# A planner's list that knows a shared SBUF path, and where the low parts of w_in are made

## The chip, the cores and the metric

One core of a Trainium2 chip runs the whole program in one launch. The metric is the device time in microseconds, the median over runs; three runs of the kernel before gave 571.86 us (569.98 to 573.15). The engines are TensorE (PE), VectorE (DVE), ScalarE (ACT), GpSimd (POOL) and SyncE (SP, which here only issues DMAs).

## The reference

For 4 batches of 8 heads, 576 tokens and 64 columns per head, the program computes causal attention and adds a linear-memory term, and then runs a two-layer network over all 2304 tokens:

```
scores = where(causal, -1e9, q @ k.T / sqrt(D));  a = exp(scores - max)
local  = (a / (a.sum(-1) + 1e-9)) @ v
q_p    = where(q > 0, q, exp(q) - 1) + 1
mem    = (q_p @ M_prev) / (q_p . z_prev + 1e-6)
x      = g * mem + (1 - g) * local            # g = sigmoid(beta), per head
out    = (s * relu(x @ w_in)**2 + b) @ w_out  # 512 -> 2048 -> 512
```

The weights come as 64-bit floats and are turned into 32-bit ones on the chip. Products with w_in and w_out use a high and a low part of each operand (three products in place of one).

## The kernel before

Sixteen pairs of heads (g = 0 to 15, four pairs to a batch) go through the same stages. For a pair, the scores of five row tiles (`scores`, L319) go to PSUM; `red` (L327, the instruction is at L330) adds the mask on VectorE, copies the tile to SBUF and keeps its extreme in `mn`; `ex` (L334, L336) is ScalarE's exponential, which leaves the row sum in `sm`; L367 adds 1e-9 to the sums and L368 takes reciprocals, both on VectorE; `scale` (L339, L342) multiplies each tile on GpSimd by its reciprocal and by 1 - g. Meanwhile `phi` (L262 to L292) makes the memory term's left side: two activations on ScalarE, a combination on VectorE (L275), a product with z on GpSimd (L277), its sum (L279), a small product and a reciprocal (L280, L283) on VectorE, and the normalised result on GpSimd (L287). TensorE then transposes the scaled tiles (`bank`, L383, instruction at L392), ScalarE and VectorE copy them out of PSUM (`copy`, L396 to L409), and the second product (`second`, L425, L435) yields x, which L456 (ScalarE) and L457 (VectorE) split into a high and a low part.

`convert` (L465) does w_in in 20 pieces of 128 rows, eight of 256 columns and twelve of 512. A piece is loaded by SP (L479); ScalarE takes the absolute value of the high word (L481); three VectorE instructions shift and merge the bits (L482, L483, L485); GpSimd makes the high part (L487); and the low part, the difference (L489), is made on GpSimd for the first 16 pieces (`WP = 16`) and on VectorE for the last four. Three raw buffers and two work buffers are taken in turn.

When a batch of x is there, `first` (L506) adds its products with w_in (L496 to L498), 41 tiles in all, as work that TensorE can do between the stages of later pairs. These use the full array ("full"), scores and transposes use it by rows ("row"), the second product by columns ("col").

The order of all this work is written by the class `Plan` (L42). Each step is added with its engine, an assumed cost, a rank, what it reads and writes and which PSUM buffers it takes and gives. `deal` (L72) plays the steps through with these costs: it keeps a clock for each engine, picks the engine that can start first and, of the steps that can start within 0.02 us, the one of lowest rank. For TensorE it keeps to the present kind of product, except that it leaves "full" when other work has waited `HOLD` us or amounts to `WORK` us. The steps are then issued in the order of their assumed starts, and each engine runs its instructions in that order, waiting at each for what it needs. Costs are only used for the order: the chip takes its own times. The copy's and the reduction's ranks are made earlier by UC and UR, and the ranks of the pieces are in `WRANK`.

After the last pair come the remaining products with w_in, and then the layer with w_out (L581 on), which the change does not touch.

Of the kernel before, what the change touches and what calls it, by code (L numbers as in the profile page):

```python
# [8 lines left out]
F32 = mybir.dt.float32  # L9
# [32 lines left out]
class Plan:  # L42
# [6 lines left out]
    RATE = 220.0e3  # L49
    SWITCH, HOLD, WORK = 0.14, 1.0, 2.0  # L50

# [3 lines left out]

    def add(self, eng, cost, fn, rank, reads=(), writes=(), take=(), give=(), bytes=0, mode=None, slack=0.0):
        s = dict(eng=eng, cost=cost, fn=fn, rank=rank, take=take, give=give, bytes=bytes, mode=mode, slack=slack,
                 n=len(self.steps), out=[], end=None)
        deps = {self.wrote[k]["n"]: self.wrote[k] for k in (*reads, *writes) if k in self.wrote}
        for k in writes:  # L60
            deps |= {r["n"]: r for r in self.read.pop(k, ())}
            self.wrote[k] = s
        for k in reads:
            self.read.setdefault(k, []).append(s)
        s["need"] = len(deps)
        s["deps"] = list(deps.values())
        for d in s["deps"]:
            d["out"].append(s)
        self.steps.append(s)
        return s  # L70

    def deal(self):  # L72
        ready = {}
        clock = {}
        wire = 0.0
        mode = None
# [10 lines left out]
        while any(ready.values()):  # L87
            best = None
            for eng, some in ready.items():
                t0 = clock.get(eng, 0.0)  # L90
                able = []
                for s in some:
                    t = max(t0, s["at"])
                    for place, pool in s["take"]:
                        if place is not None:
                            free = sorted(x for x in self.free[pool] if x is not None)
                            n = sum(1 for q in s["take"] if q[1] == pool)
                            t = max(t, free[n - 1] + s["slack"]) if len(free) >= n else None
                            break
                    if t is not None:  # L100
                        able.append((t, s))
# [21 lines left out]
            if s["eng"] == "PE":  # L123
                t += self.SWITCH * (s["mode"] != mode)
                mode = s["mode"]
            s["end"] = clock[s["eng"]] = t + s["cost"]
            if s["bytes"]:
                wire = max(wire, t) + s["bytes"] / self.RATE
                s["end"] = wire + 1.9
# [17 lines left out]
def attention_moe_kernel(  # L147
# [83 lines left out]
    NRM = two([128, 5, 2, 1], "nrm")  # L231
    MN, SM = two([128, 2, 5], "mn"), two([128, 2, 5], "sm")
    PR = two([128, 2, 1920], "P")
# [9 lines left out]
    def setup():  # L243
        nc.gpsimd.memset(mask, 0.0)
        for r, c in ((slice(0, 128), slice(448, 576)), (slice(0, 64), slice(576, 640)), (slice(64, 128), slice(576, 640))):
            nc.gpsimd.affine_select(
                out=mask[r, c], in_=mask[r, c], pattern=[[-1, c.stop - c.start]],
                compare_op=ALU.is_ge, fill=NEG, base=0, channel_multiplier=1,
            )
        nc.vector.memset(omg, 0.0)  # L250
        nc.scalar.activation(omg, omg, AF.Exp)
        for _ in range(WARM):
            nc.tensor.transpose(TB[3][:, :128], ident, ident)
# [5 lines left out]
    COLD, WARM = 1.2, 13  # L259
    UR, UC, UX = 0.6, 0.5, 1.0  # L260

    def phi(g):  # L262
# [11 lines left out]
        add("ACT", 0.72, lambda: nc.scalar.activation(q, q, AF.Exp), r0 + 0.61, [], [("q", u)])  # L274
        add("DVE", 0.80, lambda: nc.vector.scalar_tensor_tensor(q, q, 1.0, PHR, ALU.min, ALU.add), r0 + 0.7,  # L275
            ["phr"], [("q", u)])
        add(vec[0], 1.6 if own else 0.83, lambda: vec[1].tensor_mul(  # L277
            PHR, q, z.unsqueeze(1).to_broadcast([128, 5, 2, D])), r0 + 0.71, [("q", u), ("z", u)], ["phr"])
        add("DVE", 0.80, lambda: nc.vector.tensor_reduce(n, PHR, AX.X, ALU.add), r0 + 0.72, ["phr"], [("n", u)])  # L279
        add("DVE", 0.18, lambda: nc.vector.scalar_tensor_tensor(  # L280
            n, n, 1e-6, gin[:, hp:hp + 2].unsqueeze(1).unsqueeze(3).to_broadcast([128, 5, 2, 1]), ALU.add, ALU.mult),
            r0 + 0.73, ["gin"], [("n", u)])
        add("DVE", 0.2, lambda: nc.vector.reciprocal(n, n), r0 + 0.74, [], [("n", u)])  # L283

        def put(a, w, ts):
            o = P[:, :, a:].rearrange("q j (t c) -> q t j c", c=w)[:, :, :, 0:64]
            vec[1].tensor_mul(o, q[:, ts], n[:, ts].to_broadcast(list(o.shape)))  # L287

        add(vec[0], 0.85 if own else 0.5, lambda: put(0, 640, slice(2, 5)), r0 + 0.75, [("q", u), ("n", u)],
            [("phi", u, i) for i in (2, 3, 4)])  # L290
        add(vec[0], 0.62 if own else 0.4, lambda: put(384, 768, slice(1, None, -1)), r0 + 0.76, [("q", u), ("n", u)],
            [("phi", u, i) for i in (0, 1)])  # L292

    RED = (0.15, 0.27, 0.41, 0.54, 0.68)
    EXP = (0.34, 0.44, 0.55, 0.67, 0.77)
    SCL = ((0.38, 0.56, 0.7, 0.9, 0.96), (0.37, 0.5, 0.62, 0.78, 0.86))

    def attention(g):
# [3 lines left out]
        cold = 1.0 if own else COLD  # L302
        qk, P, mn, sm, V, xs = QK[u], PR[u], MN[u], SM[u], VS[u], XS[g % 8]
        add = plan.add
# [29 lines left out]
        def ex(i, j):  # L334
            pt = P[:, j, PB[i] + 64:PB[i] + 64 + QW[i]]
            nc.scalar.activation(  # L336
                pt, pt, AF.Exp, scale=-1.0, bias=mn[:, j, i:i + 1], accum_out=sm[:, j, i:i + 1])

        def scale(i, j):  # L339
            h = 2 * p + j  # L340
            pt = P[:, j, PB[i] + 64:PB[i] + 64 + QW[i]]
            nc.gpsimd.tensor_scalar(pt, pt, sm[:, j, i:i + 1], omg[:, h:h + 1], ALU.mult, ALU.mult)  # L342

# [5 lines left out]
        for v, group in enumerate(visits):  # L349
# [7 lines left out]
            for k, (i, o) in enumerate(tiles):  # L357
                for j in range(2):
                    last = k == len(tiles) - 1
                    add("DVE", RED[i], lambda i=i, j=j, o=o, ps=ps: red(i, j, o, ps), r + 0.1 + 0.01 * k - UR,  # L360
                        [("sc", g, v)], [("p", u, i, j), ("mn", u, i, j)], give=[(ps, j, "S")] if last else ())
                    add("ACT", EXP[i], lambda i=i, j=j: ex(i, j), r + 0.15 + 0.01 * k, [("mn", u, i, j)],
                        [("p", u, i, j), ("sm", u, i, j)])
            a, z = parts[v]
            keys = [("sm", u, i, j) for i in range(a, z) for j in range(2)]
            s = sm[:, :, a:z]
            add("DVE", 0.17, lambda s=s: nc.vector.tensor_scalar(s, s, 1e-9, None, ALU.add), r + 0.6, [], keys)  # L367
            add("DVE", 0.2, lambda s=s: nc.vector.reciprocal(s, s), r + 0.6, [], keys)  # L368
            for k, i in enumerate(i for i in (3, 1, 2, 0, 4) if a <= i < z):
                for j in range(2):  # L370
                    add("POOL", SCL[g >= 6][i], lambda i=i, j=j: scale(i, j), r + 0.7 + 0.01 * k,
                        [("sm", u, i, j), "omg"], [("p", u, i, j)])

# [37 lines left out]
        for q, k in enumerate((0, 3, 1, 2)):  # L411
# [6 lines left out]
            for h in range(2):  # L418
                add("DVE" if k == 3 else "ACT", 0.39 if k == 3 else 0.49, lambda k=k, h=h, ps=ps: copy(k, h, ps),
                    r + 0.1 - UC, [("tp", g, k)], [("pt", u if k > 1 else 2, h, k)], give=[(ps, h, "T")])  # L420
# [22 lines left out]
        for hi in (None,) if own else range(2):  # L443
# [3 lines left out]
            for n, (a, z) in enumerate(cuts):  # L447
# [4 lines left out]
                else:  # L452
# [4 lines left out]
                add("DVE", w + 0.03, lambda t=t, d=d: nc.vector.tensor_sub(d[:, 1], t(), d[:, 0].bitcast(F32)),  # L457
                    r0 + 2.3 - UX, [("av", g)] + key(0), key(1),
                    give=() if n < len(cuts) - 1 else [(ps, 0, "S") if own else (ps, hi, "T")])
# [5 lines left out]
    def convert(n):  # L465
# [7 lines left out]
        A, B_ = ("xa", n % 3), ("w", n % 2)  # L473
        k = (0.1 + 0.9 * n_ / 512)

        def add(eng, cost, *a):
            plan.add(eng, cost * k, *a)

        plan.add("SP", 0.06, lambda: nc.sync.dma_start(raw, words(w_in)[128 * p:128 * p + 128, c0:c0 + n_]),  # L479
                 rank - 3.0, writes=[A], bytes=1024 * n_)  # L480
        add("ACT", 0.65, lambda: nc.scalar.activation(w, hi.bitcast(F32), AF.Abs, scale=2.0 ** -112), rank, [A], [B_])  # L481
        add("DVE", 0.73, lambda: nc.vector.tensor_scalar(wu, wu, 3, None, ALU.logical_shift_left), rank, [], [B_])  # L482
        add("DVE", 0.95, lambda: nc.vector.scalar_tensor_tensor(  # L483
            wu, lo, 29, wu, ALU.logical_shift_right, ALU.bitwise_or), rank, [A], [B_])
        add("DVE", 0.72, lambda: nc.vector.scalar_tensor_tensor(  # L485
            wu, hi, 0x80000000, wu, ALU.bitwise_and, ALU.bitwise_or), rank, [A], [B_])
        add("POOL", 0.8, lambda: nc.gpsimd.tensor_scalar(H, w, 1.0, 1.0, ALU.mult, ALU.mult), rank, [B_], [("WH", n)])  # L487
        low = ("POOL", 1.35, nc.gpsimd) if n < WP else ("DVE", 0.8, nc.vector)
        add(*low[:2], lambda: low[2].tensor_sub(L, w, H.bitcast(F32)), rank, [B_, ("WH", n)], [("WL", n)])  # L489

# [43 lines left out]
    def flush():  # L534
# [4 lines left out]
    MM = [(b, f) for b in range(B - 1) for f in range(NF - LEFT * (b == 2))]  # L539
    WP = 16  # L540
    WRANK = [5.0, 6.6, 7.0, 7.2] + [9.0 + 0.2 * k for k in range(4)] + [10.0 + 0.2 * k for k in range(4)] + [
        12.0 + 0.6 * k for k in range(8)]

# [304 lines left out]
```

## Time and profile before

| | |
|---|---|
| Median of three runs | 571.86 us (569.98 to 573.15) |
| Profiled execution, time | 569.1 us |
| Profiled execution, span | 567.3 us |
| Mean granted clock of TensorE | 0.985 |
| Busy: PE / DVE / ACT / POOL | 543.0 / 357.0 / 398.4 / 319.7 us |
| L342 (scaling), GpSimd | 160 instructions, 113.1 us |
| L330 (reduction), VectorE | 160 instructions, 70.0 us |
| L336 (exponential), ScalarE | 160 instructions, 88.5 us |

The profiled execution lies at the lower end of the runs. Its busy times count an engine as busy while an instruction that it has begun waits for a resource, which matters where two engines share one. The span falls into the attention stage (to about 300 us) and the layer with w_out.

### The profile page before, as it was taken

The page shows a single profiled execution, that of the slowest core. Times are in us where ns is not written, and L with a number is a line of the kernel's source. Part 1 is how long each engine was busy: PE and PEld are TensorE (multiplying, and loading weights), DVE is VectorE, ACT ScalarE, POOL GpSimd, SP SyncE. Part 2 cuts the span into 40 slices and gives each one's busy share as a digit, 9 for nine tenths or more (in the row PEclk, how much of TensorE's full clock was granted, in tenths as well). Part 3 has the DMA queues.
Part 4 walks back from the last instruction along what each step waited for, and adds up shares of the span by engine and source line. Part 5 has one row for each costly group of instructions (what it writes and reads, how often), then busy time and mean ns, then how long its engine had stood idle before and what let it go on. Part 6 is the DMA issues. An engine that isn't in the chain of part 4 may idle for free.

```text
span 567.3 us, 11900 instructions
## 1 busy us (share of the span) xinstructions
PE 543.0 (96%) x4309; PEld 457.8 (81%) x4309; DVE 357.0 (63%) x868; ACT 398.4 (70%) x869; POOL 319.7 (56%) x341
## 2 busy tenths in 40 slices
PE   5987998999999999999999999999999999999996
PEld 4756765667777776777778888889999999999996
DVE  4887996897666544105305996346856886687562
ACT  5898876577787677226634675968789779877940
POOL 3699989985894665104400000143687687768850
PEclk9898998999999999999999999999999999999999
DMA  5635567573425443221119666648353535343101
GB/s 174 213 103 182 165 198 235 167 207 123 149 90 163 132 147 106 80 94 56 40 55 325 224 198 192 213 140 268 104 169 110 162 121 164 106 147 123 38 29 38
DMA packets 56666, 81.52 MB, mean 144 GB/s; under 512 B 7584, under 2 KB 39072, under 8 KB 56608
## 3 DMA queue, kind: packets, MB, share of 16 engines
q1 hardware_dynamic: 54592, 78.93, 43.5%
q10 hardware_dynamic: 2016, 1.84, 0.9%
q8 instruction: 34, 0.56, 0.4%
q14 instruction: 24, 0.20, 0.1%
HBM read 57.15 MB, written 23.59 MB: 142 GB/s over the span
## 4 chain that ended last, share of the span: by engine, by line
PE 64%; DVE 9%; POOL 9%; DMA 7%; ACT 7%; issue 3%; SPq 1%; ACTq 0%; POOLq 0%; DVEq 0%
PE yps L709 11%; PE yps L711 11%; PE yps L710 11%; PE tb L496 6%; PE sb L435 5%; PE sb L323 5%; PE tb L498 5%; PE tb L497 5%; DMA raw<-in_moe_w_out_dram 5%; POOL P L342 4%; PE tb L392 3%; DVE P L330 2%; ACT P L336 2%; POOL w0L L489 1%; DMA r_d<-r 1%
## 5 line engine op out<-in xcount | busy, mean ns | idle before, releaser
L342 POOL TENSOR_SCALAR P<-P,sm,omg 128x192 f32<-128x192 f32 (+4 forms) x160 | 113.1, 720 | 63.3 <-DVE sm L368 44.1
L336 ACT ACTIVATE P<-P,mn 128x64 f32<-128x64 f32 (+4 forms) x160 | 88.5, 562 | 24.1 <-DVE mn L330 23.9
L709 PE MATMUL yps<-bH,op 128*128 128x256 f32 x360 | 101.2, 281 | 0.0
L711 PE MATMUL yps<-bH,op 128*128 128x256 f32 x360 | 101.1, 281 | 0.0
L710 PE MATMUL yps<-bL,op 128*128 128x256 f32 x360 | 101.1, 281 | 0.0
L330 DVE CUSTOM_DVE_ANT_0 P<-sb,mask 128x320 f32<-128x320 f32 (+4 forms) x160 | 70.0, 483 | 36.8 <-PE sb L323 34.7
L695 POOL TENSOR_TENSOR sum<-w0L 128x512 f32<-128x512 f32 x20 | 30.4, 1519 | 106.8 <-ACT w0L L675 82.8
L323 PE MATMUL sb<-qk 64*128 64x288 f32 (+4 forms) x384 | 62.8, 437 | 5.6 <-DVE mn L330 5.6
L710 PEld LDWEIGHTS yps<-bL,op 128*128 128x128 f32 x360 | 67.9, 189 | 0.0
L711 PEld LDWEIGHTS yps<-bH,op 128*128 128x128 f32 x360 | 67.9, 189 | 0.0
L709 PEld LDWEIGHTS yps<-bH,op 128*128 128x128 f32 x360 | 67.8, 188 | 0.0
L392 PEld LDWEIGHTS tb<-ident,P 64*128 64x128 f32 x928 | 39.3, 142 | 26.6 <-issue 8.1
L323 PEld LDWEIGHTS sb<-qk 64*128 64x128 f32 x384 | 41.6, 201 | 18.4 <-DVE mn L330 8.6
L392 PE MATMUL tb<-ident,P 64*128 64x64 f32 x928 | 45.9, 232 | 10.9 <-POOL P L287 3.2
L517 ACT ACTIVATE r<-tb 128x512 f32<-128x512 f32 x41 | 24.3, 593 | 32.8 <-PE tb L498 28.7
L701 POOL TENSOR_TENSOR op<-w0L,op 128x512 fp32r<-128x512 f32 x30 | 42.1, 1418 | 5.0 <-ACT op L700 4.8
L695 POOL TENSOR_TENSOR sum<-w1L 128x512 f32<-128x512 f32 x16 | 24.4, 1525 | 30.9 <-DVE op L701 26.8
L496 PE MATMUL tb<-xs,w0H 128*128 128x512 f32 x96 | 41.6, 433 | 0.2 <-ACT pt L402 0.2
L700 ACT CAST op<-w0L 128x512 fp32r<-128x512 f32 x50 | 30.0, 616 | 16.1 <-DVE w0L L699 8.6
L709 PE MATMUL yps<-w0H,op 128*128 128x256 f32 x144 | 40.7, 283 | 0.0
L710 PE MATMUL yps<-w1H,op 128*128 128x256 f32 x144 | 40.7, 283 | 0.0
L711 PE MATMUL yps<-w0H,op 128*128 128x256 f32 x144 | 40.7, 283 | 0.0
(136 smaller groups left out, 1451.7 us busy)
## 6 DMA issues: line engine op xcount, KB each, us to landing
r_d<-r SPq DMA_DIRECT2D x41, 256.0 KB, 2.2
w0L<-r_d SPq DMA_DIRECT2D x20, 512.0 KB, 4.7
qk<-in_qk_t_dram SPq DMA_DIRECT2D x15, 576.0 KB, 4.4
raw<-in_moe_w_out_dram SPq DMA_DIRECT2D x16, 512.0 KB, 5.6
w1L<-r_d SPq DMA_DIRECT2D x16, 512.0 KB, 4.8
xa<-in_moe_w_in_dram SPq DMA_DIRECT2D x12, 512.0 KB, 4.1
r_d<-r SPq DMA_DIRECT2D x48, 128.0 KB, 1.8
qs<-in_q_rows_dram SPq DMA_DIRECT2D x16, 320.0 KB, 3.7
```

What stands on the lines that cost most here:

```text
L323: nc.tensor.matmul(SB[ps[j]][:, o:o + n], lhsT=qk[rs, 128 * i:128 * i + 128], rhs=qk[rs, S + 64 + c0:S + 64 + c0 + n], start=True, stop=Tr ...
L330: nc.vector.tensor_tensor_reduce(P[:, j, PB[i] + 64:PB[i] + 64 + n], SB[ps[j]][:, o:o + n], m, -SCALE, 3.0e38, ALU.add, ALU.min, mn[:, j, ...
L336: nc.scalar.activation(pt, pt, AF.Exp, scale=-1.0, bias=mn[:, j, i:i + 1], accum_out=sm[:, j, i:i + 1])
L342: nc.gpsimd.tensor_scalar(pt, pt, sm[:, j, i:i + 1], omg[:, h:h + 1], ALU.mult, ALU.mult)
L392: nc.tensor.transpose(TB[ps[h]][:, o[h]:o[h] + 64], P[rs, j, c:c + 128], ident[rs, rs], tile_position=(64 * h, 0))
L496: nc.tensor.matmul(ps, lhsT=wH[:, p, fs], rhs=xs[:, 0], start=p == 0, stop=False)
L695: nc.gpsimd.tensor_sub(x, y, A[{7: 21, 3: 11}[m]])
L700: nc.scalar.copy(H, x)
L701: (nc.gpsimd if m in ONPOOL else nc.vector).tensor_sub(L, x, H.bitcast(F32))
L709: nc.tensor.matmul(ps, lhsT=H, rhs=BH, start=f == 0, stop=False)
L710: nc.tensor.matmul(ps, lhsT=H, rhs=BL, start=False, stop=False)
L711: nc.tensor.matmul(ps, lhsT=L, rhs=BH, start=False, stop=f == KF - 1)
```

## The change

`Plan.add` gets a mark `port`, which GpSimd's steps always carry and on VectorE those given it: L275, L280, L482, L483, L485 and L489. `deal` keeps one clock for all marked steps: a marked step starts no earlier than the end of the last marked one, less a small `FREE`. Assumed costs are replaced throughout. HOLD goes from 1.0 to 1.5, UR from 0.6 and UC from 0.5 to 1.0, and WRANK is changed. The last reduction of a score buffer, and the last low part of x, are made to follow the earlier ones in the list, since they give the buffer back. All 20 low parts of w_in are made on VectorE. The row sums get a second column that holds 1e-9 from the start, and one reduction over two columns, into a new tile `sr`, takes the place of the addition.

```
-    SWITCH, HOLD, WORK = 0.14, 1.0, 2.0
+    SWITCH, HOLD, WORK = 0.14, 1.5, 2
+    FREE = {"DVE": 0.05, "POOL": 0.10}
...
-                    t = max(t0, s["at"])
+                    t = max(t0, s["at"], port if s["port"] else 0.0)
...
+            if s["port"]:
+                port = max(port, s["end"] - self.FREE[s["eng"]])
...
-    MN, SM = two([128, 2, 5], "mn"), two([128, 2, 5], "sm")
+    MN, SM, SR = two([128, 2, 5], "mn"), two([128, 2, 5, 2], "sm"), two([128, 2, 5], "sr")
...
+        for t in SM:
+            nc.gpsimd.memset(t, 1e-9)
...
-    UR, UC, UX = 0.6, 0.5, 1.0
+    UR, UC, UX = 1.0, 1.0, 1.0
...
-        add("DVE", 0.80, lambda: nc.vector.scalar_tensor_tensor(q, q, 1.0, PHR, ALU.min, ALU.add), r0 + 0.7,
-            ["phr"], [("q", u)])
+        add("DVE", 0.73, lambda: nc.vector.scalar_tensor_tensor(q, q, 1.0, PHR, ALU.min, ALU.add), r0 + 0.7,
+            ["phr"], [("q", u)], port=True)
...
-    RED = (0.15, 0.27, 0.41, 0.54, 0.68)
-    EXP = (0.34, 0.44, 0.55, 0.67, 0.77)
-    SCL = ((0.38, 0.56, 0.7, 0.9, 0.96), (0.37, 0.5, 0.62, 0.78, 0.86))
+    RED = (0.14, 0.27, 0.41, 0.54, 0.68)
+    EXP = (0.33, 0.44, 0.55, 0.66, 0.77)
+    SCL = (0.37, 0.48, 0.59, 0.70, 0.80)
...
-                        [("sc", g, v)], [("p", u, i, j), ("mn", u, i, j)], give=[(ps, j, "S")] if last else ())
+                        [("sc", g, v)] + ([("rd", g, v, j, q) for q in range(k)] if last else []),
+                        [("p", u, i, j), ("mn", u, i, j), ("rd", g, v, j, k)], give=[(ps, j, "S")] if last else ())
...
-            add("DVE", 0.17, lambda s=s: nc.vector.tensor_scalar(s, s, 1e-9, None, ALU.add), r + 0.6, [], keys)
-            add("DVE", 0.2, lambda s=s: nc.vector.reciprocal(s, s), r + 0.6, [], keys)
+            s, t = sm[:, :, a:z], sr[:, :, a:z]
+            add("DVE", 0.08, lambda s=s, t=t: nc.vector.tensor_reduce(t, s, AX.X, ALU.add), r + 0.6, keys, inv)
+            add("DVE", 0.12, lambda t=t: nc.vector.reciprocal(t, t), r + 0.6, [], inv)
...
-        low = ("POOL", 1.35, nc.gpsimd) if n < WP else ("DVE", 0.8, nc.vector)
-        add(*low[:2], lambda: low[2].tensor_sub(L, w, H.bitcast(F32)), rank, [B_, ("WH", n)], [("WL", n)])
+        add("DVE", 0.6, lambda: nc.vector.tensor_sub(L, w, H.bitcast(F32)), rank, [B_, ("WH", n)], [("WL", n)], fixed=0.1, port=True)
...
-    WP = 16
-    WRANK = [5.0, 6.6, 7.0, 7.2] + [9.0 + 0.2 * k for k in range(4)] + [10.0 + 0.2 * k for k in range(4)] + [
-        12.0 + 0.6 * k for k in range(8)]
+    WRANK = [5, 6.6, 6.5, 7.5] + [8.5 + 0.1 * k for k in range(4)] + [12.0 + 0.1 * k for k in range(4)] + [
+        10.0 + 0.4 * k for k in range(8)]
```

## Rows read from the trace of the kernel before

**Rows 1.** The page's slices: busy tenths of TensorE.
```profile
PE   5987998999999999999999999999999999999996
```

**Rows 2.** Windows: stretch, length, busy of PE, PEld, DVE, ACT, POOL; clock, DMA.
```profile
20.00:68.00 48.00, 41.11 (x463) 31.19 (x464) 42.00 (x155) 45.18 (x138) 43.67 (x62) 0.93 0.50 154
68.00:140.00 72.00, 66.14 (x529) 47.39 (x527) 61.98 (x150) 50.84 (x130) 63.23 (x68) 0.98 0.63 191
140.00:300.00 160.00, 159.63 (x1280) 117.30 (x1277) 65.61 (x237) 97.15 (x251) 73.60 (x104) 1.00 0.31 102
```

**Rows 3.** Waits of TensorE: total us, times, longest.
```profile
PE sb L323 <- DVE mn L330: 5.6, 7, 2.1
PE tb L392 <- POOL P L287: 3.2, 3, 1.2
PE tb L392 <- POOL P L342: 1.9, 4, 0.7
```

**Rows 4.** Chain of waits by line, 20 to 40 us, then 40 to 140.
```profile
by line: ACT P L336 32.9%; PE sb L323 13.4%; PE tb L435 11.9%; ACT F L404 10.9%; issue 7.7%; ACT pt L402 7.5%; PE tb L392 5.2%; DVE P L330 3.3%; DVE xs L457 3.3%; ACT phr L273 3.1%; ACT xs L456 1.4%; DVE x L457 1.1%; ACT x L456 0.5%; DVE mn
...
by line: POOL P L342 23.4%; DVE P L330 9.8%; POOL w0L L489 7.7%; issue 7.2%; POOL P L287 6.1%; DVE w L483 4.4%; DVE w L485 4.2%; POOL w0H L487 3.6%; POOL phr L277 3.5%; POOL w1H L487 2.8%; PE tb L392 2.8%; DVE w L482 2.7%; DMA z<-in_z_prev_
```

**Rows 5.** Timeline from 67 us (start, us, instruction); L275's durations min/median/max, ns.
```profile
67.17 2.08 DVE L275 SCALAR_TENSOR_TENSOR qs<-qs,phr 128x640 f32<-128x640 f32 x1
...
67.85 0.72 POOL L489 TENSOR_TENSOR w0L<-w,w0H 128x256 fp32r<-128x256 f32 x1
...
68.56 1.40 POOL L342 TENSOR_SCALAR P<-P,sm,omg 128x576 f32<-128x576 f32 x1
...
L275 DVE SCALAR_TENSOR_TENSOR qs<-qs,phr x16: 803/826/2081, 10.8 to 222.5; 128x640 f32<-128x640 f32 x16
```

**Rows 6.** L489: busy of DVE and POOL by windows; durations; VectorE's idle before it.
```profile
0.00:68.00 68.00, 0.00 (x0) 3.74 (x5) 0.90 0.54 164
68.00:140.00 72.00, 2.69 (x3) 13.86 (x12) 0.98 0.63 191
...
L489 POOL TENSOR_TENSOR w0L<-w,w0H x12: 723/796/1790, 33.1 to 97.0; 128x256 fp32r<-128x256 f32 x8, 128x512 fp32r<-128x512 f32 x4
L489 POOL TENSOR_TENSOR w1L<-w,w1H x4: 1268/1292/1429, 102.6 to 119.1; 128x512 fp32r<-128x512 f32 x4
L489 DVE TENSOR_TENSOR w1L<-w,w1H x4: 681/682/1324, 124.1 to 142.5; 128x512 fp32r<-128x512 f32 x4
...
  POOL w1H L487: 0.5, 1
```

**Rows 7.** L367 by windows; durations of L367 and L279, min/median/max.
```profile
0.00:68.00 68.00, 3.50 (x11) 0.90 0.54 164
68.00:140.00 72.00, 1.68 (x7) 0.98 0.63 191
...
L367 DVE TENSOR_SCALAR sm<-sm x33: 106/174/847, 7.8 to 276.2; 128x2 f32<-128x2 f32 x16, 128x8 f32<-128x8 f32 x15, 128x4 f32<-128x4 f32 x2
...
L279 DVE TENSOR_REDUCE nrm<-phr x16: 768/808/821, 14.0 to 228.7; 128x10 f32<-128x640 f32 x16
```

**Rows 8.** Timeline from 86.5 us: ScalarE's unpacking, TensorE's next instruction.
```profile
86.56 0.67 ACT L481 ACTIVATE w<-xa 128x512 f32<-128x512 f32 x1 [3.88 <-POOL w0L L489]
...
88.94 0.49 PE L392 MATMUL tb<-ident,P 64*128 64x64 f32 x9 [1.92 <-ACT r L517]
```

**Rows 9.** Timeline of TensorE: first and last of 47 entries into full-array products.
```profile
68.47 0.50 PE L496 MATMUL tb<-xs,w0H 128*128 128x512 f32 x1
68.80 0.40 PE L497 MATMUL tb<-xs,w0H 128*128 128x512 f32 x1
69.04 0.39 PE L498 MATMUL tb<-xs,w0L 128*128 128x512 f32 x1
...
291.32 0.50 PE L496 MATMUL tb<-xs,w0H 128*128 128x512 f32 x1
```

**Rows 10.** Waits of SP's queue, 0 to 140 us.
```profile
SPq L479 <- DVE w L485: 25.1, 12, 4.3
```

More of the change, by code (lines that the diff above doesn't have):

```diff
@@ L54, in __init__, with add @@
         self.free = {k: [0.0] * n for k, n in pools.items()}
-    def add(self, eng, cost, fn, rank, reads=(), writes=(), take=(), give=(), bytes=0, mode=None, slack=0.0):
-        s = dict(eng=eng, cost=cost, fn=fn, rank=rank, take=take, give=give, bytes=bytes, mode=mode, slack=slack,
+    def add(self, eng, cost, fn, rank, reads=(), writes=(), take=(), give=(), bytes=0, mode=None, slack=0.0, port=False):
+        s = dict(eng=eng, cost=cost, fn=fn, rank=rank, take=take, give=give, bytes=bytes, mode=mode, slack=slack, port=port or eng == "POOL",
                  n=len(self.steps), out=[], end=None)
@@ L74, in deal @@
         clock = {}
-        wire = 0.0
+        wire = port = 0.0
         mode = None
@@ L274, in phi @@
         add("ACT", 0.72, lambda: nc.scalar.activation(q, q, AF.Exp), r0 + 0.61, [], [("q", u)])
-        add("DVE", 0.80, lambda: nc.vector.scalar_tensor_tensor(q, q, 1.0, PHR, ALU.min, ALU.add), r0 + 0.7,
-            ["phr"], [("q", u)])
-        add(vec[0], 1.6 if own else 0.83, lambda: vec[1].tensor_mul(
+        add("DVE", 0.73, lambda: nc.vector.scalar_tensor_tensor(q, q, 1.0, PHR, ALU.min, ALU.add), r0 + 0.7,
+            ["phr"], [("q", u)], port=True)
+        add(vec[0], 1.54 if own else 0.83, lambda: vec[1].tensor_mul(
             PHR, q, z.unsqueeze(1).to_broadcast([128, 5, 2, D])), r0 + 0.71, [("q", u), ("z", u)], ["phr"])
-        add("DVE", 0.80, lambda: nc.vector.tensor_reduce(n, PHR, AX.X, ALU.add), r0 + 0.72, ["phr"], [("n", u)])
-        add("DVE", 0.18, lambda: nc.vector.scalar_tensor_tensor(
+        add("DVE", 0.73, lambda: nc.vector.tensor_reduce(n, PHR, AX.X, ALU.add), r0 + 0.72, ["phr"], [("n", u)])
+        add("DVE", 0.08, lambda: nc.vector.scalar_tensor_tensor(
             n, n, 1e-6, gin[:, hp:hp + 2].unsqueeze(1).unsqueeze(3).to_broadcast([128, 5, 2, 1]), ALU.add, ALU.mult),
-            r0 + 0.73, ["gin"], [("n", u)])
-        add("DVE", 0.2, lambda: nc.vector.reciprocal(n, n), r0 + 0.74, [], [("n", u)])
+            r0 + 0.73, ["gin"], [("n", u)], port=True)
+        add("DVE", 0.13, lambda: nc.vector.reciprocal(n, n), r0 + 0.74, [], [("n", u)])
         def put(a, w, ts):
@@ L287, in put @@
             vec[1].tensor_mul(o, q[:, ts], n[:, ts].to_broadcast(list(o.shape)))
-        add(vec[0], 0.85 if own else 0.5, lambda: put(0, 640, slice(2, 5)), r0 + 0.75, [("q", u), ("n", u)],
+        add(vec[0], 0.80 if own else 0.5, lambda: put(0, 640, slice(2, 5)), r0 + 0.75, [("q", u), ("n", u)],
             [("phi", u, i) for i in (2, 3, 4)])
-        add(vec[0], 0.62 if own else 0.4, lambda: put(384, 768, slice(1, None, -1)), r0 + 0.76, [("q", u), ("n", u)],
+        add(vec[0], 0.58 if own else 0.35, lambda: put(384, 768, slice(1, None, -1)), r0 + 0.76, [("q", u), ("n", u)],
             [("phi", u, i) for i in (0, 1)])
-    RED = (0.15, 0.27, 0.41, 0.54, 0.68)
-    EXP = (0.34, 0.44, 0.55, 0.67, 0.77)
-    SCL = ((0.38, 0.56, 0.7, 0.9, 0.96), (0.37, 0.5, 0.62, 0.78, 0.86))
+    RED = (0.14, 0.27, 0.41, 0.54, 0.68)
+    EXP = (0.33, 0.44, 0.55, 0.66, 0.77)
+    SCL = (0.37, 0.48, 0.59, 0.70, 0.80)
     def attention(g):
@@ L302, in attention @@
         cold = 1.0 if own else COLD
-        qk, P, mn, sm, V, xs = QK[u], PR[u], MN[u], SM[u], VS[u], XS[g % 8]
+        qk, P, mn, sm, sr, V, xs = QK[u], PR[u], MN[u], SM[u], SR[u], VS[u], XS[g % 8]
         add = plan.add
@@ L336, in ex @@
             nc.scalar.activation(
-                pt, pt, AF.Exp, scale=-1.0, bias=mn[:, j, i:i + 1], accum_out=sm[:, j, i:i + 1])
+                pt, pt, AF.Exp, scale=-1.0, bias=mn[:, j, i:i + 1], accum_out=sm[:, j, i, 0:1])
         def scale(i, j):
@@ L341, in scale @@
             pt = P[:, j, PB[i] + 64:PB[i] + 64 + QW[i]]
-            nc.gpsimd.tensor_scalar(pt, pt, sm[:, j, i:i + 1], omg[:, h:h + 1], ALU.mult, ALU.mult)
+            nc.gpsimd.tensor_scalar(pt, pt, sr[:, j, i:i + 1], omg[:, h:h + 1], ALU.mult, ALU.mult)
         visits = SCORES0 if g == 0 else SCORES
@@ L365, in attention @@
             keys = [("sm", u, i, j) for i in range(a, z) for j in range(2)]
-            s = sm[:, :, a:z]
-            add("DVE", 0.17, lambda s=s: nc.vector.tensor_scalar(s, s, 1e-9, None, ALU.add), r + 0.6, [], keys)
-            add("DVE", 0.2, lambda s=s: nc.vector.reciprocal(s, s), r + 0.6, [], keys)
+            inv = [("sr", u, i, j) for i in range(a, z) for j in range(2)]
+            s, t = sm[:, :, a:z], sr[:, :, a:z]
+            add("DVE", 0.08, lambda s=s, t=t: nc.vector.tensor_reduce(t, s, AX.X, ALU.add), r + 0.6, keys, inv)
+            add("DVE", 0.12, lambda t=t: nc.vector.reciprocal(t, t), r + 0.6, [], inv)
             for k, i in enumerate(i for i in (3, 1, 2, 0, 4) if a <= i < z):
                 for j in range(2):
-                    add("POOL", SCL[g >= 6][i], lambda i=i, j=j: scale(i, j), r + 0.7 + 0.01 * k,
-                        [("sm", u, i, j), "omg"], [("p", u, i, j)])
+                    add("POOL", SCL[i], lambda i=i, j=j: scale(i, j), r + 0.7 + 0.01 * k,
+                        [("sr", u, i, j), "omg"], [("p", u, i, j)])
         def load_v():
@@ L418, in attention @@
             for h in range(2):
-                add("DVE" if k == 3 else "ACT", 0.39 if k == 3 else 0.49, lambda k=k, h=h, ps=ps: copy(k, h, ps),
+                add("DVE" if k == 3 else "ACT", (0.33 if h == 0 else 0.46) if k == 3 else 0.48, lambda k=k, h=h, ps=ps: copy(k, h, ps),
                     r + 0.1 - UC, [("tp", g, k)], [("pt", u if k > 1 else 2, h, k)], give=[(ps, h, "T")])
@@ L457, in attention @@
                 add("DVE", w + 0.03, lambda t=t, d=d: nc.vector.tensor_sub(d[:, 1], t(), d[:, 0].bitcast(F32)),
-                    r0 + 2.3 - UX, [("av", g)] + key(0), key(1),
+                    r0 + 2.3 - UX, [("av", g)] + key(0) + [("cut", g, hi, q) for q in range(n)], key(1) + [("cut", g, hi, n)],
                     give=() if n < len(cuts) - 1 else [(ps, 0, "S") if own else (ps, hi, "T")])
@@ L473, in convert, with add @@
         A, B_ = ("xa", n % 3), ("w", n % 2)
-        k = (0.1 + 0.9 * n_ / 512)
-        def add(eng, cost, *a):
-            plan.add(eng, cost * k, *a)
+        k = n_ / 512
+        def add(eng, cost, *a, fixed=0.08, port=False):
+            plan.add(eng, fixed + (cost - fixed) * k, *a, port=port)
         plan.add("SP", 0.06, lambda: nc.sync.dma_start(raw, words(w_in)[128 * p:128 * p + 128, c0:c0 + n_]),
                  rank - 3.0, writes=[A], bytes=1024 * n_)
[L481 to L487, printed above, removed]
-        low = ("POOL", 1.35, nc.gpsimd) if n < WP else ("DVE", 0.8, nc.vector)
-        add(*low[:2], lambda: low[2].tensor_sub(L, w, H.bitcast(F32)), rank, [B_, ("WH", n)], [("WL", n)])
+        add("ACT", 0.58, lambda: nc.scalar.activation(w, hi.bitcast(F32), AF.Abs, scale=2.0 ** -112), rank, [A], [B_])
+        add("DVE", 0.34, lambda: nc.vector.tensor_scalar(wu, wu, 3, None, ALU.logical_shift_left), rank, [], [B_], port=True)
+        add("DVE", 0.61, lambda: nc.vector.scalar_tensor_tensor(
+            wu, lo, 29, wu, ALU.logical_shift_right, ALU.bitwise_or), rank, [A], [B_], port=True)
+        add("DVE", 0.61, lambda: nc.vector.scalar_tensor_tensor(
+            wu, hi, 0x80000000, wu, ALU.bitwise_and, ALU.bitwise_or), rank, [A], [B_], port=True)
+        add("POOL", 0.6, lambda: nc.gpsimd.tensor_scalar(H, w, 1.0, 1.0, ALU.mult, ALU.mult), rank, [B_], [("WH", n)])
+        add("DVE", 0.6, lambda: nc.vector.tensor_sub(L, w, H.bitcast(F32)), rank, [B_, ("WH", n)], [("WL", n)], fixed=0.1, port=True)
     def mm1(ps, b, f, half):
```

## Prediction

> **What bounds the kernel now.** I read the forty slices first. TensorE (PE) reads 9 in all but some slices of the first quarter and the very last one [rows 1]. So two regimes: from about 140 us TensorE is full, and what another engine gains there moves nothing; before, it has holes. The table of windows sizes them: stage A, 20 to 68 us (no product with w_in has begun yet), PE busy 41.11 of 48.00, 6.9 us idle, at a mean granted clock of 0.93; stage B, 68 to 140 us, 66.14 of 72.00, 5.9 us idle, at 0.98; stage C, 140 to 300 us, 0.4 us idle at 1.00. GpSimd (POOL) is busy 43.67 us in A and 63.23 in B, but 73.60 of 160 in C: where it is nearly full, TensorE is not [rows 2]. Granted clock below 1 is time at the lower of two levels (1.2 instead of 2.4 GHz): 0.07 x 48 = 3.4 us and 0.02 x 72 = 1.4 us of full-speed work. TensorE's holes in A and B with this loss, 17.6 us, are all that the change can give back, apart from switches between kinds of product (below).
>
> The waits of TensorE name who makes the holes: scores that wait for the masked reductions on VectorE (DVE) to free a PSUM buffer, 5.6 us; transposes that wait for GpSimd's phi products (3.2) and scalings (1.9) [rows 3]. The chain of waits says who is late behind them: from 20 to 40 us ScalarE's exponentials lead (32.9%) and GpSimd does not appear among the lines shown; from 40 to 140 us the leading entries are GpSimd's scaling (23.4%), VectorE's reduction (9.8%) and GpSimd's low parts of w_in (7.7%), with VectorE's unpacking behind them [rows 4].
>
> Last I looked at whether the two engines stand in each other's way. At 67.17 VectorE is given L275 (0.803 us at its shortest) and it shows 2.08 us, over a scaling and a low part on GpSimd; it ends at 69.25. GpSimd's next scaling starts at 68.56 and takes 1.40, ending 0.7 us after VectorE let go [rows 5]. One waits for the other, both count the wait as busy, so "busy" is not demand. The Trainium skill, "SBUF — State Buffer", section "Who interferes with whom", has this as an exclusive lock held for the whole instruction, by VectorE instructions with two SBUF inputs against GpSimd ones that read SBUF; the trace agrees, 2.08 us against 0.803.
>
> **The change part by part.**
> Low parts: 16 of 20 pieces leave GpSimd, 5 in A (3.74 us) and 12 in the window of B (13.86 us; one lies across the border) [rows 6]. On VectorE a 512-wide one takes 0.68 us undisturbed against 1.27 on GpSimd, from the four that are there already [rows 6]. A 256-wide one is not shown on VectorE: between 0.34 (half) and 0.68; I take 0.41, a half plus a little fixed cost, against 0.72 on GpSimd. A: 3.74 - 5 x 0.41 = 1.7 us of the shared resource freed. B: 4 narrow and 8 wide, 13.86 - (4 x 0.41 + 8 x 0.68 = 7.1) = 6.8 us freed. By the skill's lock rule the 7.1 us still exclude GpSimd, as I count them; without it the whole 13.86 us would be freed, and TensorE's 5.9 us of holes would cap the gain all the same.
>
> New wait: each moved low part stands in VectorE's in-order queue behind GpSimd's high part (L487). Behind it stand reductions, and TensorE's scores and ScalarE's exponentials wait for those. The four that exist cost 0.5 us of idle in all [rows 6]. I put 0.1 us on each, inside the sums' roundings; the other end is among the rivals. In return ScalarE's unpacking no longer waits for GpSimd to release the work buffer, which cost it 3.88 us before 86.56 us, with TensorE then idle for 1.92 us before 88.94 [rows 8].
>
> Sum with 1e-9: 33 tensor_scalar on VectorE with a median of 0.174 and up to 0.847 us go, 33 reductions over two columns come [rows 7]. The new one is not shown; from below the shortest of the old (0.106), from above the reduction of 640 columns (0.81) [rows 7]. I take 0.12, since the operands are as tiny as the old one's. A: 3.50 - 11 x 0.12 = 2.2 us of VectorE; B: 1.68 - 7 x 0.12 = 0.8 us. The long reductions keep to 0.768 to 0.821 us over 16 runs, so nothing of GpSimd's delays them [rows 7]. The 15 left, in C, lie beside a full TensorE: nothing. The two memsets at the start lie in GpSimd's wait for the gate: nothing; without that cover some 0.2 us (estimate).
>
> The list: knowing the exclusion, measured costs and earlier ranks (UR, UC) put every engine's instructions in another order. No row shows the new order. Its gain is bounded by the holes in B, where products with w_in stood ready behind a waiting transpose; its loss by nothing in a row, and the nearest are holes of one to two microseconds each. I count it inside the term for B. HOLD 1.5 lets fewer, longer runs of full-array products form: entering one costs 0.33 us to its second product where the next step takes 0.24, so with leaving some 0.2 us each (estimate); of 47 entries, from 68.47 to 291.32 us, perhaps ten merge [rows 9], so 0 to 2 us; I take 0.5.
>
> Loads of w_in: their ranks move, but all 20 stay on SP in order. SP stood 25.1 us for VectorE to release raw buffers [rows 10], with loads for attention queued behind; VectorE's release comes sooner or later with its own order. None of the waits that make TensorE's holes names a DMA, so I count nothing; a late load would show as such a wait.
>
> The sum. A: 1.7 + 2.2 = 3.9 us freed, about half reaches TensorE, since up to 40 us ScalarE leads: -2.0 (0 to -5.3, with 1.4 of clock). B: 6.8 + 0.8 = 7.6 us freed, but holes plus clock hold 7.3; of the holes those behind GpSimd or the unpacking are some 3.5, with 0.5 of clock: -4.0 (0 to -7.3). Switches: -0.5. Total -6.5. The profiled execution took 569.1 us (567.3 of span and 1.8 around it), so 562.6 in its terms. The median of the three runs, 571.86, lies 2.8 above it: 565.4.
>
> **The rivals.**
> *Nothing moves.* The Trainium skill, "Perfetto Trace Analysis", section "Optimizing Scalar/DVE Operations", warns that moving work between these two engines may not help, as they share a port. As a mechanism here: VectorE, busy 61.98 of 72 in B, gets 7.1 us more and loses 0.8, its reductions come later by what GpSimd's scalings come earlier, and TensorE's holes change owner. For it: VectorE's share of the chain. Against: 0.68 instead of 1.27 us a piece frees time for both. Time: 569 to 575 on the median's scale.
>
> *VectorE becomes the bound: slower.* In B its load is 61.98 + 7.1 - 0.8 = 68.3 of 72 us. Twelve low parts that each wait more than (72 - 68.3) / 12 = 0.31 us for their high part fill it, and from there every wait is TensorE's. At 0.6 us each, as when L487 stands behind a scaling, B grows by 12 x 0.6 - 3.7 = 3.5 us, A by about 1: 573.6, or 576.4 on the median's scale. Against: part of the 61.98 is lock waiting that shrinks, and the present four wait 0.1 each.
>
> *More than I forecast.* If the new order closes B whole (7.3), A gives its 5.3 and switches 2, it is -14.6: 557.3 on the median's scale. Against: A's start is ScalarE's.
>
> **How the numbers follow.** Forecast, 562 to 569: 0.50. More, 557 to 562: 0.15. Nothing, 569 to 575: 0.20. Slower, above 575: 0.15. What a measurement here can tell from no change is about 0.5%, 2.9 us. Faster is the first two, 0.65; same 0.20; slower 0.15. The range of 557 to 573.5 leaves out the slower rival, a little of "nothing" and hardly anything below.
>
> **What would show it.** Right: low parts on VectorE near 0.68 us and with idle before them under 0.3 us each; GpSimd's busy time in 68 to 140 us down by ten or more; transposes' waits for GpSimd under half; PE idle from 20 to 140 us down from 12.8 to about 7 us; small reductions near 0.12 us. First product with w_in at about 66.5 instead of 68.47 us. Wrong: VectorE idle for the high part, or scores waiting longer for reductions; or the holes closed and the stretch after 140 us longer by as much.

## The result and the profile after

The changed kernel takes 563.38 us (median, 562.19 to 564.02) against 572.37 for the kernel before (median of four runs, three of which gave the 571.86 above): a ratio of 0.9863, interval 0.9834 to 0.9892. The two medians alone divide to 0.9843, inside the interval. The profiled execution took 563.7 us against 569.1; that of before lies below all its timed runs, so the profiles show 5.7 us of span and not the whole difference.

The windows of the changed kernel answer to [rows 2]; columns as there, and its first 20 us stand too:

```profile
0.00:20.00 20.00, 15.39 (x68) 11.60 (x69) 10.02 (x40) 10.81 (x29) 8.07 (x21) 1.00 0.67 201
20.00:68.00 48.00, 38.88 (x458) 29.46 (x457) 42.02 (x161) 44.64 (x136) 36.99 (x55) 0.93 0.47 137
68.00:140.00 72.00, 69.40 (x572) 52.15 (x567) 67.58 (x176) 54.31 (x137) 56.38 (x62) 1.00 0.66 203
140.00:300.00 160.00, 159.14 (x1282) 117.75 (x1281) 68.71 (x243) 99.31 (x256) 72.77 (x102) 1.00 0.36 119
```

The same window of the kernel before, 0 to 20 us:

```profile
0.00:20.00 20.00, 13.33 (x79) 10.18 (x79) 11.29 (x50) 12.35 (x34) 9.35 (x20) 0.83 0.63 190
```

In stage B (68 to 140 us) TensorE's idle time falls from 5.9 to 2.6 us and its clock reaches 1.00. Stage A (20 to 68 us) gets worse: 9.1 us idle instead of 6.9. The first 20 us show less idle time (4.6 instead of 6.7), but that is no gain: the same score products take longer there in this execution, and the first transposes start 1.5 us later. TensorE before, then after:

```profile
6.54 1.83 PE L323 MATMUL sb<-qk 64*128 64x448 f32 x8 [0.86 <-DVE mn L330]
...
17.22 0.31 PE L392 MATMUL tb<-ident,P 64*128 64x64 f32 x1
```

```profile
7.16 3.21 PE L328 MATMUL sb<-qk 64*128 64x448 f32 x8 [0.86 <-DVE mn L335]
...
18.69 0.31 PE L399 MATMUL tb<-ident,P 64*128 64x64 f32 x1
```

The change does not decide this: of the runs below, two with the old list start these transposes at 17.24 (e2) and 18.49 us (e5), and one with the new list at 16.64 (e1). The granted clock does not tell it either (0.83 before, 1.00 after). The cause stays open, and the 1.5 us are to be taken off when later times of the two profiles are compared.

Waits of TensorE, whole span:

```profile
PE tb L399 <- POOL P L292: 3.6, 1, 3.6
PE sb L328 <- DVE mn L335: 2.7, 3, 1.4
...
PE tb L399 <- POOL P L347: 1.1, 3, 0.4
```

Against [rows 3], scores wait half as long for the reductions, but one hole of 3.6 us behind GpSimd's phi products (now L292) is new. It ends at 34.30 us, in stage A; here is the reciprocal that the phi products need, GpSimd, and TensorE behind it (timeline):

```profile
27.29 0.17 DVE L288 RECIPROCAL nrm<-nrm 128x10 f32<-128x10 f32 x1
...
27.74 5.14 POOL L347 TENSOR_SCALAR P<-P,sr,omg 128x448 f32<-128x448 f32 x8
...
32.85 1.40 POOL L292 TENSOR_TENSOR P<-qs,nrm 128x384 f32<-128x384 f32 x2
...
34.30 0.52 PE L399 MATMUL tb<-ident,P 64*128 64x64 f32 x9 [3.57 <-POOL P L292]
```

The new list has put eight scalings ahead of a pair of phi products whose last input was ready at 27.46. No run tried them the other way round. The first product with w_in comes later than before, not earlier (68.47 in [rows 9]); of the 2.3 us, 1.5 are those of the start:

```profile
70.74 0.50 PE L502 MATMUL tb<-xs,w0H 128*128 128x512 f32 x1
```

The low parts (now L495), durations min/median/max in ns and VectorE's idle time before them, against [rows 6]:

```profile
L495 DVE TENSOR_TENSOR w0L<-w,w0H x12: 411/620/1091, 28.5 to 100.1; 128x256 fp32r<-128x256 f32 x8, 128x512 fp32r<-128x512 f32 x4
L495 DVE TENSOR_TENSOR w1L<-w,w1H x8: 672/681/1279, 106.4 to 138.1; 128x512 fp32r<-128x512 f32 x8
...
  POOL w0H L494: 0.6, 1
  POOL w1H L494: 0.5, 1
```

The sums (now L374) by windows and durations, against [rows 7]:

```profile
0.00:68.00 68.00, 1.68 (x11) 0.95 0.53 156
68.00:140.00 72.00, 1.18 (x8) 1.00 0.66 203
...
L374 DVE TENSOR_REDUCE sr<-sm x33: 99/158/173, 8.5 to 280.5; 128x2 f32<-128x4 f32 x16, 128x8 f32<-128x16 f32 x15, 128x4 f32<-128x8 f32 x2
```

The prices were right: 0.41 and 0.68 us for a low part at its shortest, and waits for high parts of 1.1 us over 20 pieces. The new sum never exceeds 0.173 us where the addition reached 0.847.

### The profile page after: what moved, and what is told of

The parts are those of the page before. It is cut to its first block, busy times and chain, and to the rows that moved or that the text cites. A ratio compares the mean times of both kernels' runs of the same rounds, so it can differ in the third digit from the quotient of the medians.

```text
span 561.6 us, 11890 instructions
## 1 busy us (share of the span) xinstructions
PE 540.5 (96%) x4309; PEld 458.6 (82%) x4309; DVE 357.9 (64%) x884; ACT 399.4 (71%) x869; POOL 304.4 (54%) x327
## 4 chain that ended last, share of the span: by engine, by line
PE 87%; ACT 4%; DVE 4%; POOL 2%; issue 1%; POOLq 0%; ACTq 0%; DVEq 0%
PE yps L714 11%; PE yps L715 11%; PE yps L716 11%; PE sb L328 8%; PE tb L502 8%; PE tb L503 7%; PE tb L504 7%; PE sb L442 6%; PE hps L502 5%; PE hps L503 5%; PE hps L504 5%; PE tb L399 4%; ACT P L341 2%; DVE P L335 2%; POOL P L347 1%
## 5 line engine op out<-in xcount | busy, mean ns | idle before, releaser
L347 POOL TENSOR_SCALAR P<-P,sr,omg 128x192 f32<-128x192 f32 (+4 forms) x160 | 113.1, 724 | 58.0 <-DVE sr L375 37.4
L335 DVE CUSTOM_DVE_ANT_0 P<-sb,mask 128x64 f32<-128x64 f32 (+4 forms) x160 | 69.8, 483 | 39.9 <-PE sb L328 39.8
L409 ACT COPY pt<-tb 128x512 f32<-128x512 f32 x64 | 34.4, 589 | 11.0 <-PE tb L399 10.7
L502 PE MATMUL tb<-xs,w0H 128*128 128x512 f32 x96 | 40.4, 420 | 0.8 <-ACT pt L409 0.3
L714 PE MATMUL yps<-w0H,op 128*128 128x256 f32 x144 | 40.7, 283 | 0.0
```

The source lines that it names most:

```text
L335: nc.vector.tensor_tensor_reduce(P[:, j, PB[i] + 64:PB[i] + 64 + n], SB[ps[j]][:, o:o + n], m, -SCALE, 3.0e38, ALU.add, ALU.min, mn[:, j, ...
L347: nc.gpsimd.tensor_scalar(pt, pt, sr[:, j, i:i + 1], omg[:, h:h + 1], ALU.mult, ALU.mult)
L502: nc.tensor.matmul(ps, lhsT=wH[:, p, fs], rhs=xs[:, 0], start=p == 0, stop=False)
L714: nc.tensor.matmul(ps, lhsT=H, rhs=BH, start=f == 0, stop=False)
```

## The experiments

Theory "work": the gain is GpSimd's and VectorE's time on the shared path, freed by the moved low parts and the sums. Theory "order": it is the new list. Ratios are to the kernel before on the same chip, with 95% intervals.

| run | list | work | ratio |
|---|---|---|---|
| changed kernel | new | new | 0.9863 [0.9834, 0.9892] |
| e1 | new order kept | old | 1.0014 [0.9995, 1.0033] |
| e2 | old order kept | new | 0.9861 [0.9835, 0.9888] |
| e5 | old order kept | low parts only | 0.9872 [0.9848, 0.9896] |
| e6 | old order kept | sums only | 0.9994 [0.9976, 1.0011] |
| e7 | old order kept | new, high parts on ScalarE | 0.9898 [0.9864, 0.9932] |
| e8 | old list dealt anew | new | 1.0115 [1.0090, 1.0140] |
| e3 | new, no exclusion | new | 1.0201 [1.0173, 1.0229] |
| e9 | new, HOLD 1.0 | new | 0.9868 [0.9845, 0.9891] |
| e10 | new, FREE 0 | new | 1.0005 [0.9986, 1.0024] |
| e11 | new, UR and UC old | new | 0.9885 [0.9862, 0.9907] |
| e12 | as e11, no exclusion | new | 1.0152 [1.0130, 1.0173] |
| e4 | new, low parts on GpSimd | sums new | 1.0418 [1.0389, 1.0446] |

**e1 and e2: order against work.** "Order kept" means that the list is dealt with one set of engines and only the engine that does the step is another.

```
e1, on the changed kernel:
-  nc.vector.tensor_sub(L, w, H...)
+  (nc.gpsimd if n < 16 else nc.vector).tensor_sub(L, w, H...)
-  nc.vector.tensor_reduce(t, s, AX.X, ALU.add)
+  nc.vector.tensor_scalar(t, s[:, :, :, 0], 1e-9, None, ALU.add)
e2, on the kernel before (and the two-column sum as in the change):
-  low[2].tensor_sub(L, w, H...)
+  nc.vector.tensor_sub(L, w, H...)
```

> The new list in its new order, but the work as before: the first 16 low parts of w_in run on GpSimd and 1e-9 is added by a tensor_scalar. Theory 'order' (the gain is the new list): ratio to before about 0.988, some -7 us. Theory 'work' (the gain is the 7 us of GpSimd time and the small reductions): about 1.000, or slower, as the list now counts on a low part on VectorE. My prediction's terms put most on the work: about 0.998.

> The old list in its old order, with the new work: all low parts on VectorE and 1e-9 through a sum over two columns. Theory 'order': ratio about 0.998. Theory 'work': about 0.990, -6 us. If VectorE is held by waits for high parts, slower: 1.005.

The new order with the old work gains nothing; the old order with the new work gains all of it. "Order" falls. (e1's list was made for low parts on VectorE, so by itself it could be unfair to the new order; but with the new work the new order is no better than the old one.) The windows of e2, stages A and B:

```profile
20.00:68.00 48.00, 40.46 (x467) 30.32 (x468) 43.63 (x161) 46.31 (x142) 42.31 (x59) 0.96 0.51 151
68.00:140.00 72.00, 70.34 (x568) 50.28 (x567) 63.26 (x172) 52.38 (x131) 54.71 (x61) 1.00 0.65 202
```

and its TensorE waits for GpSimd, and the first product with w_in:

```profile
PE tb L394 <- POOL P L289: 1.6, 1, 1.6
PE tb L394 <- POOL P L344: 0.8, 2, 0.5
```

```profile
67.23 0.50 PE L498 MATMUL tb<-xs,w0H 128*128 128x512 f32 x1
```

Here is most of the picture that I forecast: B's holes 5.9 to 1.7 us at full clock, transposes' waits for GpSimd 5.1 to 2.4 us, the first product with w_in 1.2 us sooner (with the first transposes level, 17.24 and 17.22). Only the idle time in A does not fall: 7.5 us instead of 6.9, at a clock of 0.96 instead of 0.93. The span is 8.0 us shorter than before (559.3).

**e5 and e6: which part of the work.** e5 makes only e2's first edit, e6 only the two-column sum.

> The kernel before in its old order, with only the low parts of w_in moved to VectorE; 1e-9 is added as before. If the gain of the new work is the GpSimd time of the low parts: ratio to before 0.989. If it is the small reductions: 0.998. By my terms (low parts 1.7 and 6.8 us freed of 3.9 and 7.6): about 0.990.

> The kernel before in its old order, with only the sum over two columns in place of the addition of 1e-9; low parts as before. If the small steps' waiting for GpSimd matters: 0.992. By my terms (2.2 and 0.8 us of VectorE freed): about 0.997.

The low parts are the gain; of the sums nothing can be measured, and my 0.997 for them lies just outside the interval.

Moving a low part does two things at once. It takes time off the path that the two engines share, and it gives the work buffer back to ScalarE's unpacking sooner. Who waited for the low parts, before and in e5 (total us, times):

```profile
  ACT w L481: 8.2, 5
```

```profile
  ACT w L481: 2.6, 4
```

TensorE's waits before, 68 to 140 us, hold both kinds of hole, the first behind the unpacking [rows 8] and the other two behind GpSimd:

```profile
PE tb L392 <- ACT r L517: 1.9, 1, 1.9
PE tb L392 <- POOL P L342: 1.6, 3, 0.7
PE tb L392 <- POOL P L287: 1.0, 1, 1.0
```

In e5 the first is gone and 0.7 us are left of the others, in e2 0.5. So both kinds closed with the one move; no run makes the one without the other.

**e7: is the shared path still the bound?** On e2:

```
-  nc.gpsimd.tensor_scalar(H, w, 1.0, 1.0, ALU.mult, ALU.mult)
+  nc.scalar.copy(H, w)
```

> Old order with all the new work, and the 20 high parts of w_in made by ScalarE's copy instead of GpSimd. If the time of GpSimd and VectorE on the shared path bounds 20 to 140 us: a further 0.004 to 0.008 below the run with the new work alone (0.986), so about 0.980. If the gain of that run was ScalarE's earlier unpacking, or ScalarE is now what is late: 0.986 or above.

Stage B of e7:

```profile
68.00:140.00 72.00, 68.27 (x564) 49.88 (x563) 64.70 (x169) 59.45 (x145) 40.60 (x44) 1.00 0.63 200
```

GpSimd is busy 40.60 us instead of 54.71, and TensorE has 3.7 us of holes instead of 1.7. TensorE's waits in this stretch:

```profile
PE sb L437 <- DVE mn L332: 2.3, 2, 1.7
PE sb L325 <- DVE mn L332: 0.8, 1, 0.8
PE tb L394 <- DVE F L408: 0.5, 1, 0.5
```

None is for GpSimd or ScalarE: what is late is now VectorE. (The six times lie in two groups, 561.4 to 561.7 and 565.7 to 566.2; the profile is of the lower, level with e2.) The 0.980 did not come: once the low parts are off, freeing more of GpSimd gives nothing, and there is little left to win. ScalarE, busy 59.45 us instead of 52.38, may be why VectorE is late; that was not tried. So e7 does not confirm the shared path as what the low parts freed. By its expectation, ScalarE's earlier unpacking stays possible as the source of e2's gain, in whole or in part.

**e3, e8, e9 to e12: what the exclusion in the list is worth.** e3: `port=False` for every step. e8: e2 with `WP = 0`, so that the old list plans VectorE for the low parts and comes out in another order. e9: `HOLD = 1.0`. e10: `FREE` zero. e11: `UR, UC = 0.6, 0.5`. e12: e11 with `port=False`.

> The changed kernel with one thing undone: no step is marked, so the list does not know that the two engines exclude each other; costs, ranks and work are the new ones. If the exclusion in the list carries the gain: ratio to before about 0.998. If the work and the other constants carry it: 0.988, as the changed kernel (0.986).

> The new work (low parts on VectorE, two-column sum) dealt anew by the old list: old costs, ranks and HOLD, no exclusion; only the low part's engine and cost (0.8 us) are told to it. If a list that is to be dealt anew needs to know the exclusion: 1.00 or above, as the changed kernel without it (1.020). If the old, longer costs stand in for it: about 0.986, as with the old order kept.

> The changed kernel with HOLD back at 1.0, dealt anew with the exclusion known. If knowing the exclusion makes good lists: 0.985 to 0.990, plus up to 0.002 for more switches. If the changed kernel's list is one good deal among scattered ones: anywhere from 0.985 to 1.02.

> The changed kernel with FREE at zero: the exclusion is known but for 0.05 and 0.10 us at the end of a step. If knowing the exclusion makes good lists: 0.985 to 0.990. If the list is one good deal: scattered up to 1.02.

> The changed kernel with UR and UC back at 0.6 and 0.5. If knowing the exclusion makes good lists: 0.985 to 0.990; if reductions and copies that go first are part of the gain: 0.990 to 0.995; if deals scatter: up to 1.02.

> The run with UR and UC as before, with the exclusion taken out of the list too: a second pair beside the changed kernel with and without it (0.986 and 1.020). If knowing the exclusion is worth something as such: 0.01 or more above its partner. If those two were two deals of a scatter: no steady sign, from 0.985 to 1.02.

All these kernels do the same work. Dealt with the exclusion known, the four lists give 0.9863, 0.9868, 0.9885 and 1.0005; dealt without, the three give 1.0115, 1.0152 and 1.0201. Two pairs differ in nothing else: 0.034 (changed kernel and e3) and 0.027 (e11 and e12). So for a list that is dealt anew, knowing it paid in both pairs, and only back to where the old order already is with the new work (e2). Two lists that both know it can differ by 1.4% (e10), so one deal's ratio says little. The old, longer costs did not stand in for it in the one deal tried (e8). TensorE from 20 to 140 us, first in the changed kernel and then in e3:

```profile
20.00:140.00 120.00, 108.28 (x1022) 81.61 (x1020) 109.60 (x336) 98.95 (x272) 93.37 (x116) 0.97 0.58 177
```

```profile
20.00:140.00 120.00, 100.82 (x897) 73.42 (x897) 105.33 (x296) 87.93 (x240) 84.19 (x110) 0.91 0.52 162
```

In e3 all engines are less busy: they wait in line. One place in its timeline shows how:

```profile
87.89 3.54 POOL L347 TENSOR_SCALAR P<-P,sr,omg 128x320 f32<-128x320 f32 x6
...
90.67 3.97 DVE L280 SCALAR_TENSOR_TENSOR qs<-qs,phr 128x640 f32<-128x640 f32 x1 [1.31 <-ACT qs L279]
91.40 1.40 POOL L292 TENSOR_TENSOR P<-qs,nrm 128x384 f32<-128x384 f32 x2
92.77 1.20 POOL L494 TENSOR_SCALAR w0H<-w 128x512 fp32r<-128x512 f32 x2
...
94.56 0.61 DVE L335 CUSTOM_DVE_ANT_0 P<-sb,mask 128x448 f32<-128x448 f32 x1
```

L280 is 0.77 us at its shortest there and takes 3.97, until GpSimd's back-to-back scaling, phi products and high parts end at 93.97; VectorE's next reduction, queued behind it, starts at 94.56. The list had counted on 0.73 us.

**e4: planned round the low parts on GpSimd.** On the changed kernel:

```
-  add("DVE", 0.6, lambda: nc.vector.tensor_sub(...), ..., fixed=0.1, port=True)
+  low = ("POOL", 1.27, nc.gpsimd, 0.16) if n < 16 else ("DVE", 0.6, nc.vector, 0.1)
+  add(*low[:2], lambda: low[2].tensor_sub(...), ..., fixed=low[3], port=True)
```

> The changed kernel with the first 16 low parts planned and run on GpSimd at their measured cost (1.27 us for 512 columns, 0.72 for 256), exclusion known. Theory 'work': the 6.8 us of GpSimd time come back in 68 to 140 us and the ratio to before is 0.994. Theory 'order': the list plans round it, 0.988.

Both theories missed. Its stage C:

```profile
140.00:300.00 160.00, 144.45 (x1139) 107.94 (x1138) 65.12 (x220) 89.18 (x231) 72.92 (x98) 0.97 0.29 92
```

TensorE has 15.5 us of holes where the changed kernel has 0.9 and no other list more than about two: this list ran 246 full-array products in one go (from 151.60 us) and had few left to set between the last pairs. The exclusion in the list is no guarantee of a good one.

None of these beats the changed kernel; e2, e5, e9 and e11 lie within its interval.

## Why the prediction was right

*Size and sign.* 565.4 forecast, 563.38 measured; forecast -6.5 us, measured 1.37%, some 7.8 us (9.0 between the medians). That the total fits so well is in part luck: the low parts gave more than I had counted for them, and the sums, HOLD and, in the changed kernel, stage A gave nothing.

*Low parts*, the largest term: right in direction, and their undisturbed prices (0.41 and 0.68 us) are what the trace shows. Alone they give 1.28%, some 7 us (e5). I had them share 6.0 with the sums; by their shares of the freed time some 4.5 of that were theirs. I had counted both time on the shared path and the earlier unpacking; how much each gave is not shown.

*Stage B, -4.0*: right in size (3.3 of idle and 1.4 of clock), and by the work, not by the list, of which I had counted some here (e1: nothing). The holes behind GpSimd and the unpacking, which I put at some 3.5, are 4.5 in the waits above.

*Stage A, -2.0*: this step failed in the changed kernel. With the old order part of it comes through (e2: the first product with w_in 1.2 us sooner, 0.03 more of clock, but no less idle time). The new list gives it away again, at one place 3.57 us of it. From the first transposes to the first product with w_in it takes 52.05 us; before it was 51.25, in e2 49.99, and in e1, the new list with the old work, 52.83. The new list must gain as much elsewhere, since it comes out even (e1). It enters full-array products 42 times instead of 47, which may be where; that is not shown.

*Sums, 3.0 us of VectorE freed*: mis-sized. One takes 0.158 us at the median and not 0.12; they cost 2.9 us up to 140 us instead of 5.2, so 2.3 are freed, but no time of the kernel (e6). The Trainium skill, "SBUF — State Buffer", section "Who interferes with whom", says that on trn2 a tensor_reduce never contends; the trace agrees (0.099 to 0.173 us over 33).

*HOLD, -0.5*: this failed too. e9 shows no difference, 0.9868, and with HOLD at 1.0 its list has the same 42 entries, so the five that went are not HOLD's.

*The new wait*: 1.1 us over 20 pieces, 0.06 us each. The rival in which VectorE becomes the bound needed 0.31. Its load in B, 67.58 us, came out near what I had worked out (68.3), in part by chance: 176 instructions fall into the window, where 162 were counted.

*"Nothing moves"*: the Trainium skill's warning ("Perfetto Trace Analysis", "Optimizing Scalar/DVE Operations") that moving work between VectorE and GpSimd might not help did not come true here: e5 gains 1.28%. The same difference takes 0.68 us on the one and 1.27 on the other.

*What I said would show it*: GpSimd's busy time in B fell by 6.9 us and not ten, as other work moved up into the window (62 instructions, where 68 less the 12 low parts would leave 56). Waits of transposes for GpSimd fell from 5.1 to 4.7 us and not by half; 3.6 of the 4.7 are the one hole in stage A. TensorE's idle time from 20 to 140 us fell from 12.8 to 11.7 and not to 7, since A's grew by 2.2 while B's fell by 3.3. In e2 the three come closer, without reaching the first and the last: 8.5 us less, 2.4 and 9.2 us.

## What to carry to other kernels

Two engines that exclude each other can be counted as one resource: add up undisturbed time on it, and try a shared step on the engine that holds it for less. Here that gave the right direction, though not the proof, since the step also released a buffer sooner. To tell a new schedule from new work, keep the old order and change only the work, and the reverse. A ratio from one freshly dealt schedule carries a scatter of a per cent or more; change one thing in pairs before believing its constants.

## What the runs showed of the hardware

In e3, VectorE's instruction with two SBUF inputs waited through five GpSimd instructions in a row (3.97 us for 0.77), not just for the one that was running: each of GpSimd's next ones began as the one before it ended, and went first. In the kernel before, L275 waited through two: the low part in [rows 5], and before that one this scaling:

```profile
67.06 0.82 POOL L342 TENSOR_SCALAR P<-P,sm,omg 128x576 f32<-128x576 f32 x1
```

In the first 17 us, eight score products of 64x448 took 1.83 us in one execution and 3.21 in another, and the granted clock of the stretch (0.83 and 1.00) did not tell which.
